# A first batch in halves of 256 tokens, early loads in another order, and a written-out list for each engine

## The chip, the cores and the metric

The kernel runs on one core of one Trainium2 chip. The metric is the device time of one execution in microseconds, the median over several. The core has a matrix engine (TensorE, PE in the profile; its weight loads are listed apart as PEld), a vector engine (DVE), a scalar engine (ACT), GpSimd (POOL) and the engine that starts most transfers (SP). Each works through its own list of instructions in order and waits on semaphores for the others. Two kinds of on-chip memory matter: SBUF, and PSUM, into which PE writes and from which DVE and ACT read.

## The reference

Attention with a feature map of exponentials, for 8 batches of 8 heads with 576 tokens of 64 features, followed by a normalised two-layer product with a residual. Cut to what matters:

```python
proj = einsum('bhsd,df->bhsf', x, w_phi)                     # 64 -> 128, for q and for k
proj = proj - max(abs(proj), axis=-1, keepdims=True)
phi  = concatenate([exp(proj), exp(-proj)], axis=-1)
kv   = einsum('bhsf,bhsd->bhfd', k_p, v);  z = sum(k_p, axis=2)
x    = einsum('bhsf,bhfd->bhsd', q_p, kv) / (einsum('bhsf,bhf->bhs', q_p, z)[..., None] + 1e-06)
x    = x.transpose(0, 2, 1, 3).reshape(8, 576, 512)
xn   = (x - mean) / sqrt(var + 1e-06) * g_ln
out  = x + maximum(xn @ w_ch1, 0.0) @ w_ch2                  # 512 -> 2048 -> 512
```

## The kernel before

**Units and groups.** The attention runs in 32 units of two heads of one batch (`NU`). Units 0 to 3 make the first 512 tokens of batch 0, units 4 to 7 those of batch 1, and so on; the last 64 tokens of each batch ("tails", "mixed", `px`) go through tiles of their own. The second part, called MoE in the code, runs over groups `g` of 512 tokens. Group 0 can start once units 0 to 3 are through. A group makes 16 first products (`first`, L1425 on: four matmuls of 512 columns into `hT_ps`, L1431, then a relu on ACT or DVE) and 4 x 16 second products (`second`, `ch_ps`, L1463). The last groups use a form with fewer multiplications (`fast`, `quick`).

**One unit.** k, q and v come in by transfers on SP. PE turns k and q (`a_trans`, L829 and L837), DVE or ACT copies them to `qkT` (L844, L846). `a_main` multiplies by `wbk`, the feature weights, with 256 columns a matmul (L984; L990 in the form for units 4 and up), DVE takes the largest absolute value over each token's 128 features (L1047, one reduction of 128 x 1024), and ACT the exponentials: for k two of 1024 into `EB` (L1067), for q two of 1024 into `EA` (L1111), the latter from a second product of q with the roles turned (`a_tails`, L999, `pt`). Small exponentials of the maxima give `ek` and `em` (L1056, L1060). `a_mixed` does the same for the 64 last tokens (`px`, L943, L944, L947, L956, L960). POOL scales v by `ek` into `vv` (L1074 to L1080), PE sums `EB` times `vv` into `n_bank` (`a_kv`, L1135, L1141), which is copied to `KV` (L1149, L1151). `a_num` multiplies `EA` by `KV` in two parts of 6 and 3 token tiles (L1199, L1205); DVE adds the two signs and takes the reciprocal of the sum (L1221, L1227, L1233), and POOL writes the quotient to `x` (L1266, L1270, "puts").

**Between the parts.** DVE takes means and variances (`x_stats` L1338, `x_center` L1350), DVE, ACT or POOL subtracts the mean (L1355, L1360, L1364), ACT makes 1/sqrt of the variance as an Ln and an Exp (`rstd`, L1370, L1371), and PE turns the result (`x_trans`, L1302) with copies on DVE or ACT (L1312, L1314). In group 0 a turn covers all four token tiles of one of four 128-wide slices, so the first product waits for all 512 tokens.

**Weights.** POOL starts the loads of w1 (L769) and w2 (L787), each in two halves, which convert to 16 bits on the way. `GATE` names the load of v that must have come before each half of w1 starts. Loads for units 8 and up wait for the half of w1 that `HOLD` names, which is half 1.

**PSUM.** Pool A has two buffers of two banks, pool B three of one bank, pool N one bank. A product waits until a buffer of its pool is free.

**The order.** Nothing is emitted as the functions run. Every function calls `add`, which records one operation: the engines that could do it, an estimate of its time, a rank, the code to emit, what it reads and writes, and which PSUM pool it takes from or gives back to. Operations are numbered in the order of these calls. At the end `Order.run` (L365 on) plays the operations through a model of the engines, picks for each free engine the waiting operation of lowest rank, and writes the instructions out in the order of that play. Ranks come from due times and from the table `OFF`, a correction for each unit and stage. While the model has no work for PE before `WARM` = 75 us, it puts in matmuls of zeros (`fill`, L2064).

## Time and profile before

| what | value |
|---|---|
| median of 3 runs | 356.31 us (356.21 to 358.39) |
| span of the profiled execution, first to last instruction | 354.4 us |
| that execution's clock of PE, as granted | 0.998 of full speed |
| transfers | 53.89 MB in 93676 packets, 152 GB/s over the span |
| bytes read and written in HBM | 36.77 MB, 9.44 MB |

The profiled execution is one run of the program. Its span reaches from the first to the last instruction, and the time of a run also holds what lies around it. A row of a timeline has the start, the duration, the engine, the line, the operation and its operands, and in brackets the idle time before it and what ended that. A row of a group has the line, engine, operation, operands, the count, the busy time, the mean duration in ns, and the idle time in front of its instructions. A row of busy time by stretch has the stretch, its length, the busy time and count of PE, PEld, DVE, ACT and POOL (those that worked), the granted clock, the share of the DMA engines and GB/s. A row of the chain has the start, the time and what it was. Instructions of one engine overlap in its pipeline, so that busy times of rows that follow each other add up to more than the time that passed.

### The profile page before, as it was taken

What the parts mean: (1) busy time and instruction counts of PE and PEld (TensorE: products, weight loads), DVE (VectorE), ACT (ScalarE), POOL (GpSimd) and SP (SyncE); (2) the same over time, 40 slices, a digit from 0 to 9 for tenths busy, and PEclk for the clock granted to TensorE, in tenths of its full rate; (3) what the DMA queues carried; (4) which work ended last, traced back from release to release, by engine and by line L of the source; (5) the groups of instructions that cost most, each with busy time, mean ns of one, the idle gap of its engine ahead of it and who ended that gap; (6) DMA issues with size and microseconds to landing.
All of it is one profiled execution on the core that took longest, in us unless ns stands there. A gap on an engine that the chain in (4) does not pass through costs nothing.

```text
span 354.4 us, 9372 instructions
## 1 busy us (share of the span) xinstructions
PE 345.6 (98%) x3606; PEld 221.1 (62%) x3632; DVE 304.8 (86%) x664; ACT 258.5 (73%) x551; POOL 189.3 (53%) x245
## 2 busy tenths in 40 slices
PE   8998999999999999999999999999999999999995
PEld 8987955556554555455545455555555578578884
DVE  5699987899987888988979989897778799999983
ACT  4997988598997996979696975787697833656410
POOL 5499755799644873747478798355546420000000
PEclk9999999999999999999999999999999999999999
DMA  7999999899996888489729242851051005400053
GB/s 210 311 215 287 210 281 246 215 235 258 294 276 175 209 185 215 115 141 280 202 68 209 72 110 47 147 153 35 2 126 63 3 7 116 123 2 3 0 120 118
DMA packets 93676, 53.89 MB, mean 152 GB/s; under 512 B 61104, under 2 KB 88048, under 8 KB 93632
## 3 DMA queue, kind: packets, MB, share of 16 engines
q1 hardware_dynamic: 89392, 47.72, 56.5%
q0 software_dynamic: 3328, 4.49, 7.1%
q10 hardware_dynamic: 912, 1.08, 0.9%
q8 instruction: 28, 0.46, 0.5%
q14 instruction: 16, 0.13, 0.1%
HBM read 36.77 MB, written 9.44 MB: 130 GB/s over the span
## 4 chain that ended last, share of the span: by engine, by line
PE 88%; DVE 8%; ACT 2%; issue 1%; DVEq 0%; ACTq 0%
PE hT_ps L1431 29%; PE ch_ps L1463 22%; PE ch L1597 9%; PE n_bank L2064 4%; PE pm L990 4%; PE n_bank L1141 4%; PE sum L1780 4%; PE num L1199 3%; PE pt L999 2%; DVE m L1047 2%; PE n_bank L1135 1%; DVE numc L1221 1%; PE n_bank L1199 1%; DVE numc L1227 1%; PE n_bank L1205 1%
## 5 line engine op out<-in xcount | busy, mean ns | idle before, releaser
L1431 PE MATMUL hT_ps<-xT,w 128*128 128x512 bf16 x496 | 118.4, 379 | 0.0
L1463 PE MATMUL ch_ps<-w,hT 128*128 128x512 bf16 x362 | 88.9, 379 | 1.3 <-issue 0.3
L1047 DVE TENSOR_REDUCE m<-pm 128x8 f32<-128x1024 f32 x64 | 76.8, 1214 | 7.1 <-PE pm L990 6.5
L1074 POOL TENSOR_TENSOR vv<-v,ek 128x1024 bf16<-128x1024 f32 x32 | 61.1, 1910 | 33.0 <-issue 18.2
L1431 PEld LDWEIGHTS <-w 128*128 128x128 bf16 x496 | 44.2, 98 | 44.0 <-issue 0.8
L1067 ACT ACTIVATE eb<-pm 128x1024 bf16<-128x1024 f32 x64 | 64.5, 1036 | 2.4 <-DVE m L1047 2.3
L1111 ACT ACTIVATE ea<-pt 128x1024 bf16<-128x1024 f32 x64 | 63.8, 1029 | 3.0 <-PE pt L999 2.7
L1266 POOL TENSOR_TENSOR x<-numc,rden 128x128 bf16<-128x128 f32 (+1 forms) x64 | 38.9, 613 | 38.6 <-DVE rden L1233 37.4
L1441 ACT ACTIVATE hT<-hT_ps 128x512 bf16<-128x512 f32 x68 | 40.6, 597 | 24.1 <-PE hT_ps L1431 23.2
L1463 PEld LDWEIGHTS <-hT 128*128 128x128 bf16 x384 | 34.0, 98 | 34.4 <-issue 0.8
L1439 DVE TENSOR_SCALAR hT<-hT_ps 128x512 bf16<-128x512 f32 x56 | 38.5, 687 | 8.6 <-PE hT_ps L1431 8.1
L1199 PEld LDWEIGHTS <-ea 128*128 128x128 bf16 x512 | 24.6, 97 | 10.5 <-issue 1.7
L1141 PE MATMUL n_bank<-vv,eb 128*128 128x65 bf16 x512 | 26.6, 194 | 0.0
L902 POOL TENSOR_TENSOR b<-qk,one 128x1024 bf16<-128x1024 f32 x11 | 20.9, 1896 | 8.9 <-DMA qkT<-b 5.5
L2064 PE MATMUL n_bank<-wz 128*128 128x120 bf16 x347 | 25.0, 224 | 0.1
L1141 PEld LDWEIGHTS <-eb 128*128 128x128 bf16 x512 | 22.3, 98 | 4.3
L1221 DVE TENSOR_TENSOR numc<-num,em 128x390 f32<-128x390 f32 (+1 forms) x40 | 20.3, 513 | 3.3 <-PE num L1199 2.5
L2064 PEld LDWEIGHTS <-wz 128*128 128x128 bf16 x347 | 21.5, 103 | 1.6 <-issue 0.5
L1480 POOL TENSOR_TENSOR o<-o,x 128x512 f32<-128x512 f32 x14 | 16.2, 1154 | 10.5 <-ACT o L1476 10.5
L1338 DVE BATCH_NORM_STATS2 st<-x 128x6 f32<-128x512 bf16 (+1 forms) x40 | 21.3, 569 | 0.4 <-POOL x L1266 0.4
L1199 PE MATMUL num<-KV,ea 128*128 128x65 bf16 x416 | 19.4, 193 | 1.6 <-ACT KV L1151 1.3
L1227 DVE TENSOR_TENSOR numc<-numc,num 128x390 f32<-128x390 f32 (+1 forms) x40 | 20.3, 516 | 0.5
(162 smaller groups left out, 608.7 us busy)
## 6 DMA issues: line engine op xcount, KB each, us to landing
out_dram<-o SPq DMA_DIRECT2D x29, 256.0 KB, 2.6
qk<-in_k_dram SPq DMA_DIRECT2D x12, 512.0 KB, 5.0
qk<-in_q_dram SPq DMA_DIRECT2D x12, 512.0 KB, 6.0
v<-in_v_dram SPq DMA_DIRECT2D x12, 512.0 KB, 4.9
w<-in_moe_w_ch_dram POOLq DMA_DIRECT2D x4, 1024.0 KB, 11.4
qk<-in_k_dram SPq DMA_DIRECT2D x8, 256.0 KB, 6.9
qk<-in_q_dram SPq DMA_DIRECT2D x7, 256.0 KB, 7.5
v<-in_v_dram SPq DMA_DIRECT2D x7, 256.0 KB, 7.4
```

The lines of the kernel that those rows point to most:

```text
L1047: nc.vector.reduce_max(out=m, in_=ps, axis=AX.X, apply_absolute_value=True)
L1067: nc.scalar.activation(eb, ps, AF.Exp, scale=(1.0, -1.0)[t])
L1074: eng.tensor_tensor(out=u["vv"][:, :, 0:MX, 0:D], in0=bcast(vb[:, hh, :].rearrange("p (c d) -> p c d", d=D), 1, 2), in1=bcast(e[:, :, 0:MX ...
L1111: nc.scalar.activation(u["EA"][:, t, 0:1024], u["pt"], AF.Exp, scale=(1.0, -1.0)[t])
L1141: nc.tensor.matmul(ps[:, t, c // 4, :], EB[:, t, c, :], vv[:, t, c, :], start=False, stop=(t == 0 and c == MX - 1), skip_group_check=True,)
L1199: nc.tensor.matmul(ps[t][:, i, :], ea(u, t, c), KV[:, t, c // 4, :], start=True, stop=True,)
L1266: eng.tensor_tensor(out=dst, in0=src, in1=by, op=ALU.mult)
L1431: nc.tensor.matmul(st["ps"], w1_sb[:, kc, jj * P : (jj + 1) * P], xT_bufs[g % XB][:, kc::KC, :], start=(kc == 0), stop=(kc == KC - 1),)
L1439: nc.vector.tensor_relu(h_sb, st["ps"])
L1441: nc.scalar.activation(h_sb, st["ps"], AF.Relu)
L1463: nc.tensor.matmul(ch[g, i], hT[g, jj][:, i * P : (i + 1) * P], w2_sb[:, jj, :], start=(jj == 0), stop=(jj == JC - 1),)
L2064: nc.tensor.matmul(warm, wz, wz[:, 0:WN], start=False, stop=False, skip_group_check=True)
```

## The change

**The order is written out.** The table `OFF` and the ranks go. In their place stands `ORDER`, which names for each engine the numbers of its operations one after the other; the model still runs, to place the filler and to merge the five lists into one program order. What `add` records for each operation is otherwise the same. The model's estimates change in many places (a table `LAG` of waits between engines, one transfer queue in place of two, other durations); they change no instruction except the number of fillers.

**Group 0 in halves.** For units 0 to 3 (`halved`), q's products go through `q_half`: two halves of 256 tokens, each with two matmuls of 256 columns in one role and two in the other in one PSUM buffer, a maximum of 128 x 512 on DVE, a small exponential and two exponentials of 512 on ACT. `num_half` takes token tiles 0, 1, 4, 5 and then 2, 3, 6, 7 with the mixed tile, in place of the parts of 6 and 3. In group 0 `x_trans_half` turns two token tiles by two slices at a time with copies of 256 columns, `rstd` is made for two tiles at a time, and `first_half` makes two first products of 256 tokens side by side in one PSUM buffer, in place of one of 512.

**Start.** Both halves of `w_phi` come by ACT's queue (one came by POOL's), q of unit 0 by SP's (it came by ACT's), the q tails of the first units are loaded as all tails are, the casts to `wbk` stand behind all the clears, and `GATE` names v of units 2 and 3 in place of 4 and 5.

The numbers of some operations of the changed kernel, counted from the calls of `add`:

| number | engine | what |
|---|---|---|
| 25 | ACT | `preload_act_table_set` |
| 85, 108, 167, 218, 273 | POOL | `vv` of units 0, 1, 2, 3, 4 |
| 154, 149 | POOL | load of w1, half 1 (slots 8 to 15) and half 0 (slots 0 to 7) |
| 168, 173 | POOL | loads of w2 |
| 130, 199, 136, 135, 205, 204, 240, 287 | POOL | puts of units 0 to 3 |
| 314, 316 | ACT, POOL | centring of token tiles 0 and 1 |
| 323, 326 | PE | `x_trans_half` of the first 256 tokens |
| 325, 327, 328, 324 | DVE, the last on ACT | their copies |
| 349, 339, 337, 343, 341 | PE | `first_half(0, 7)`, `(0, 2)`, `(0, 1)`, `(0, 4)`, `(0, 3)` |
| 374 | PE | products of q of unit 5 |
| 317, 322 | ACT | `rstd` of token tiles 0 and 1, and of 2 and 3 |
| 557, 560, 563 | PE | second products of the first token tile |
| 564 | ACT | result of the first token tile |
| 442, 465 | ACT, PE | copy of `KV` of unit 6, and the `num` that reads it |

The diff, cut to its core. The lists are cut to their first part:

```diff
-SLACK = ((0.22, 0.0, 0.0, 1.02), (0.35, 0.6, 1.6, 1.03), (0.22, -1.1, 0.0, 1.28))
+SLACK = ((0.22, 0.0, 0.0, 0.97), (0.35, 0.6, 1.6, 0.97), (0.22, -1.35, 0.0, 1.0))
...
+HALVED = 4
...
-GATE = (("v", 4), ("v", 5))
-OFF = (
...
+GATE = (("v", 2), ("v", 3))
+ORDER = {
+    "POOL": """
+        0 15 17 21 19 30 85 108 154 167 130 218 199 136 135 149 205 204 240 287 316 32 245 292
+        273 246 168 173 308 389 388 444 451 293 383 404 435 418 504 423 464 470 469 424 497 511
...
+    "SP": """
+        1 7 26 9 11 13 28 35 37 41 43 137 51 63 33 47 59 49 39 45 61 145 65 143 67 53 139 141 57
...
+    "ACT": """
+        2 72 23 98 83 99 84 93 87 94 82 119 120 97 92 79 124 106 125 105 107 118 102 123 165 166
+        164 193 194 161 192 216 215 217 188 189 187 221 212 229 230 228 278 371 234 235 233 373
+        282 413 223 314 411 271 324 272 270 267 300 350 317 377 378 338 369 331 302 303 376 275
+        305 306 307 346 362 448 364 443 447 402 356 358 403 401 409 398 352 406 429 433 434 427
+        430 432 322 564 442 25 458 459 491 457 452 575 502 494 495 496 588 526 527 524 545 599
...
+    "DVE": """
+        3 5 6 74 81 96 89 76 91 78 117 115 104 182 122 101 113 184 111 163 132 133 127 160 128
+        191 180 129 214 201 211 202 196 197 203 186 134 198 280 225 227 232 237 207 238 206 242
+        284 239 285 243 286 289 244 290 309 310 313 315 269 274 327 291 328 325 266 299 208 312
...
+    "PE": """
+        4 71 73 80 95 88 75 90 77 86 116 114 103 100 121 181 183 112 109 110 162 131 159 126 190
+        178 179 213 200 210 195 185 219 224 279 220 226 231 236 276 370 277 241 283 372 288 281
+        412 410 268 222 323 326 265 298 349 374 339 337 343 341 367 332 329 368 301 347 359 353
...
-    nc.scalar.dma_start(out=wphi_f[0:D, :], in_=w_phi)
-    nc.gpsimd.dma_start(out=wphi_f[D : 2 * D, :], in_=w_phi)
+    for i in range(2):
+        nc.scalar.dma_start(out=wphi_f[i * D : (i + 1) * D, :], in_=w_phi)
...
+    def q_half(u, h):
+        n = u["n"]
+        j = n % QB
+        st = {}
+        cs = ((0, 1, 4, 5), (2, 3, 6, 7, MX))[h]
+        nt = len(cs)
+
+        def products():
+            st["ps"] = ps = ps_A.tile([P, 2, 2, 2, P], FP32, tag="A", name="qh")
+            x = u["qkT"][:, 0:512].rearrange("p (a two t) -> p a two t", a=2, two=2)[:, :, h, :]
+            for a in range(2):
+                nc.tensor.matmul(ps[:, 0, a], x[:, a, :], wbk, start=True, stop=True)
+            for i in range(2):
+                nc.tensor.matmul(ps[:, 1, i], wbk[:, i, :], x, start=True, stop=True)
...
+    def first_half(h, j2):
+        st = {}
+
+        def products():
+            st["ps"] = ps_B.tile([P, 2, 2 * P], FP32, tag="B", name="hT_ps")
+            for k in range(2):
+                jj = 2 * j2 + k
+                for kc in range(KC):
+                    nc.tensor.matmul(
+                        st["ps"][:, k].rearrange("p (i t) -> p i t", t=P),
+                        w1_sb[:, kc, jj * P : (jj + 1) * P],
+                        xT_bufs[0][:, kc::KC, :][:, 2 * h : 2 * h + 2, :],
+                        start=(kc == 0), stop=(kc == KC - 1),
+                    )
...
-        def rstd():
-            nc.scalar.activation(rstd_x[:, g, :], mv_x[:, g, :, 1], AF.Ln, bias=eps_sb)
-            nc.scalar.activation(rstd_x[:, g, :], rstd_x[:, g, :], AF.Exp, scale=-0.5)
+        def rstd(at=slice(0, NM)):
+            nc.scalar.activation(rstd_x[:, g, at], mv_x[:, g, at, 1], AF.Ln, bias=eps_sb)
+            nc.scalar.activation(rstd_x[:, g, at], rstd_x[:, g, at], AF.Exp, scale=-0.5)
...
+        if g == 0 and i % 2:
+            add("ACT", 0.46, V, lambda: rstd(slice(i - 1, i + 1)),
+                r=[("mv", g, j) for j in (i - 1, i)], w=[("rstd", 0, i // 2)])
...
     load_main("k", 0, 1, -4.0, "SP")
-    load_main("q", 0, 1, -4.0, "ACT")
+    load_main("q", 0, 1, -4.0, "SP")
     load_tails("k", 0, -3.0, "SP")
+    load_tails("q", 0, -3.0, "POOL")
...
-            a_main(u, 0)
+            for half in range(2):
+                q_half(u, half)
```

More of the change, by code (lines that the diff above doesn't have):

```diff
@@ L393, in run @@
                 if kind == 1:
[L394 to L404 removed]
+                    offered.add(op.number)
@@ L452, in run @@
                     first, last = port[0], port[1]
-                    us = us.us + max(0.0, first - now if now < first else last - now)
-                    if now < last and any(not item[2].engine for item in waiting["POOL"]):
+                    us = us.us + max(0.0, (first if now < first else last) - now - 0.15)
+                    n = place["POOL"]
+                    if now < last and n < len(turn["POOL"]) and turn["POOL"][n] in offered:
                         us += STUCK
@@ L480, in run @@
                         offer(o)
-        assert not any(op.left or not op.engine for op in self.ops)
+        assert all(place[engine] == len(turn[engine]) for engine in turn)
         for op in done:
@@ L609 @@
         nc.vector.memset(m_, 0.0)
-    for i in range(2):
-        rows = slice(i * D, (i + 1) * D)
-        nc.vector.tensor_copy(out=wbk[rows, i, :], in_=wphi_f[rows, :])
     ea_bufs = []
```

655 lines of the change are left out of this document (286 added, 369 removed), and 99 rows, old and new, of tables (OFF, ORDER).

## The prediction

> **What bounds the kernel now.** I read the page first, then busy time by stretch, the filler's line by stretch, the chain of waits, and each engine's groups in the stretch that mattered.
>
> ```profile
> PE 345.6 (98%) x3606; PEld 221.1 (62%) x3632; DVE 304.8 (86%) x664; ACT 258.5 (73%) x551; POOL 189.3 (53%) x245
> ```
>
> PE looks full everywhere, but part of it is filler (L2064 multiplies zeros to pass the time). The first fence splits the span of 354.4 us where the first MoE product starts; the second is the filler alone in the same stretches.
>
> ```profile
> 0.00:44.60 44.60, 41.24 (x727) 38.14 (x732) 37.53 (x96) 36.57 (x83) 31.55 (x50) 1.00 1.09 246
> 44.60:354.40 309.80, 304.34 (x2880) 182.96 (x2900) 267.24 (x569) 221.97 (x470) 157.79 (x196) 1.00 0.59 138
> ```
>
> ```profile
> 0.00:44.60 44.60, 24.53 (x345) 21.30 (x345) 1.00 1.09 246
> 44.60:354.40 309.80, 0.43 (x2) 0.20 (x2) 1.00 0.59 138
> ```
>
> The columns after the stretch are PE, PEld, DVE, ACT, POOL. Before 44.6 us PE has 24.5 us of filler and 3.4 idle; after it, 0.4 and 5.5, most of that behind the last matmul. So two different bounds: up to 44.6 us PE waits for the first batch to come through DVE (37.5 of 44.6 busy) and ACT (36.6); from 44.6 on PE's own work sets the end. The chain shows the border (start, time, what):
>
> ```profile
> 43.71 0.11 PE px L943
> 43.82 0.06 PE px L944
> 43.87 0.55 PE pm L990 x16
> 44.43 0.16 PE n_bank L2064
> 44.59 0.86 PE hT_ps L1431 x4
> 45.45 0.06 PE n_bank L1135
> 45.51 0.26 PE n_bank L1141 x8
> ```
>
> Hence the sum: the new span is the start S of the first MoE product plus the PE work that is left then, plus whatever new waits appear behind S.
>
> **The change: work left at S.** The new PE list puts 54 operations ahead of its first half product (number 349, `first_half(0, 7)`). I compare them with what PE had done by 44.59 us:
>
> ```profile
> L1199 PE MATMUL num<-KV,ea 128*128 128x65 bf16 x80 | 4.3, 194 | 1.6 <-ACT KV L1151 1.3 <-ACT ea L1111 0.3
> L1141 PE MATMUL n_bank<-vv,eb 128*128 128x65 bf16 x80 | 4.0, 194 | 0.0
> L990 PE MATMUL pm<-wbk,qkT 64*128 64x128 bf16 x48 | 2.0, 217 | 0.0
> L1205 PE MATMUL num<-KV,ea 128*128 128x65 bf16 x20 | 1.8, 193 | 0.0
> L1302 PE MATMUL xT_ps<-ident,xc 128*128 128x128 bf16 x16 | 1.2, 219 | 0.0
> ```
>
> Means overlap in the pipeline, so prices come from the chain's spacing: 8 of L1141 take 0.26 (0.033 each), a 128-wide one 0.06 (L944), a 256-wide 0.11 (L943), a 512-wide 0.215 (4 of L1431 in 0.86), and L990 0.034 (16 in 0.55). By 44.59 PE had five units' num and kv; the new list has four, so 20 + 16 of 0.033 and two wider ones are still to do (1.3 us). It has one group of 16 L990 in place of three (1.1 us) and 8 transposes of x in place of 16 (0.45 us). That is 2.8 us more behind S. The halves turn 64 matmuls of 512 columns (13.8 us) into 128 of 256 (14.1 us): 0.2 more. Left behind S: 309.8 + 2.8 + 0.2 = 312.8, with the old idle and the old tail in it. Both loads of `w_phi` on ACT, the clears ahead of the casts and the preset costs in the planner change no work behind S.
>
> **When S comes: DVE.** DVE's groups up to 44.59 us:
>
> ```profile
> L1047 DVE TENSOR_REDUCE m<-pm 128x8 f32<-128x1024 f32 x13 | 15.7, 1214 | 0.5 <-PE pm L984 0.5
> L1227 DVE TENSOR_TENSOR numc<-numc,num 128x195 f32<-128x195 f32 (+1 forms) x10 | 4.4, 453 | 0.1
> L1221 DVE TENSOR_TENSOR numc<-num,em 128x195 f32<-128x195 f32 (+1 forms) x10 | 4.3, 449 | 0.1
> ...
> L947 DVE TENSOR_REDUCE m<-px 128x2 f32<-128x256 f32 x7 | 2.9, 421 | 1.0 <-PE px L944 1.0
> L1338 DVE BATCH_NORM_STATS2 st<-x 128x6 f32<-128x256 bf16 x8 | 2.9, 408 | 0.0
> L1233 DVE RECIPROCAL rden<-numc 128x3 f32<-128x3 f32 (+1 forms) x10 | 1.5, 174 | 0.0
> L1312 DVE TENSOR_SCALAR xT<-xT_ps,ngln 128x512 bf16<-128x512 bf16 x3 | 1.3, 478 | 0.1
> ```
>
> Ahead of the last copy that number 349 needs, the new DVE list has 6 whole maxima and 8 half ones (half of 1.214 and a little, 0.65) in place of 13: 3.3 us less. Eight pairs of numc and 8 rden in place of ten: 2.15 less. Four px maxima for seven: 1.25. Four stats for eight, since tokens 256 to 511 come later: 1.65. Three half copies of xT (0.3) for three whole: 0.5. Together 8.85; neighbours overlap by some 0.09 and 12 instructions fewer lose that, so 7.8, and 8.3 with small copies. That alone moves 44.6 to 36.3. DVE's gaps early on can shrink as well:
>
> ```profile
> 5.00:10.00 5.00, 4.95 (x82) 4.66 (x81) 3.82 (x9) 2.96 (x5) 0.70 (x1) 1.00 1.06 263
> 10.00:15.00 5.00, 4.95 (x79) 4.55 (x78) 3.19 (x6) 4.88 (x16) 2.61 (x3) 1.00 1.11 305
> ```
>
> 3.0 us idle there; SP now issues k and q of units 0 to 3 ahead of every v but unit 0's. No row prices that: between nothing and 3.0, I take a third. First half product: **35.3 us**. ACT's halved exponentials add some 0.3 us a unit and sit beside DVE.
>
> **When S comes: the weights.** Number 349 reads the half of w1 that POOL now loads first; the second operation behind it (339) reads the other half.
>
> ```profile
> 22.05 0.63 POOL L1080 TENSOR_TENSOR vv<-vx,ek 128x260 bf16<-128x260 f32 x1
> ...
> 24.29 1.18 POOL L1266 TENSOR_TENSOR x<-numc,rden 128x384 bf16<-128x384 f32 x2 [0.86 <-DVE rden L1233]
> ...
> 25.68 1.91 POOL L1074 TENSOR_TENSOR vv<-v,ek 128x1024 bf16<-128x1024 f32 x1
> ...
> 27.68 0.62 POOL L1080 TENSOR_TENSOR vv<-vx,ek 128x260 bf16<-128x260 f32 x1
> 28.24 0.79 POOL L769 DMA_DIRECT2D w<-in_moe_w_ch_dram  x1
> ```
>
> ```profile
> DMA to landing us min/median/max: 9.9/10.0/10.1
> ```
>
> POOL's list keeps the places: one half behind the second vv, one behind the fourth and the puts after it. A vv takes 2.6 us (25.68 to 28.3); the puts now ahead of the second half take 1.4 (two large ones took 1.18, and a small one). If the fourth vv follows the third at once (22.65), that half is issued at 26.6; with today's gaps at 28.24 + 1.4 = 29.6. With 10.0 us to land: 36.6 to 39.6. I take 36.6, since the exponentials that vv waits for also come earlier. In the meantime PE does 349 and 374 (0.86 + 0.44), so this too puts S at **35.3**. The two limits meet. w2 is issued behind five more puts, a centring and the vv of unit 4, at about 35 us by these rows and later if that vv waits for ACT; it is due behind 16 half products of 0.88 and some 4.5 us of attention work (an estimate by the same prices), at 53. A landing of 10.0 hides in that; I cost it at nothing, and one us for each us that it lands later.
>
> **A wait that the change adds.** Operation 25, the preload of ACT's tables, ran ahead of all activations. The ACT list now has it behind 97 others, both early rstd among them (numbers 317 and 322, each a Ln and then an Exp).
>
> ```profile
> 2.47 1.28 ACT L1966 ACT_TABLE_LOAD   x1 [2.47 <-issue]
> 4.54 0.58 ACT L846 COPY qkT<-qkT_ps 128x512 bf16<-128x512 bf16 x1 [0.78 <-PE qkT_ps L829]
> ```
>
> ```profile
> 44.60:60.00 15.40, 15.40 (x146) 8.52 (x146) 11.69 (x20) 12.79 (x29) 8.76 (x12) 1.00 1.22 280
> ```
>
> Something must then load tables for the first activation, and if that set has only Exp, each rstd switches twice: 4 x 1.28 = 5.1 us on ACT between the first product and the first second product. Queued behind 322 are the result of the first tile, which frees a PSUM buffer, and the KV copy of unit 6, which PE's num of unit 6 waits for. ACT had 15.40 - 12.79 = 2.6 us idle in that stretch, so 2.5 reach PE. Ends: 0 (one load serves all) and 4 x 2.07 = 8.3 (from the load's start at 2.47 to ACT's next work at 4.54) less 2.6, so 5.7. I take 2.5, by the load's own row. The Trainium skill ("ScalarE: Activation LUTs", Table sets: the hidden batching unit) lists a set with exp alone beside one with exp and ln, and says that a load is placed before an activation whose function is not loaded; by that the four switches happen, while the trace of before, with one load ahead of everything, can't show it. The same page (What ACT_TABLE_LOAD costs) gives 1.28 us for the load, as the row has it, and 2.66 with a drain; by 2.66 the sum below would be 358.0 instead of 352.5.
>
> **Sum.** 35.3 + 312.8 + 2.5 = 350.6 us of span. The profiled execution has 354.4 against the median of 356.31, so 1.9 lie around it: **352.5 us**, 1.1% below. One per cent (3.6 us) is about what a measurement of this kernel tells from no change.
>
> **The rivals.**
> 1. The tables cost PE nothing, because one set serves or ACT loads while PE waits for w1: 35.3 + 312.8 + 1.9 = 350.0; with DVE's whole early gap closed (2 us more, weights keeping up) 348.0. For it: ACT's 2.6 us of idle time; against it: the two rstd stand ahead of the preload.
> 2. Each switch holds ACT longer than its row, up to the 2.07 above: 350.0 + 5.7 = 355.7, within 1%. PE then waits longer at num of unit 6. The Trainium skill's page "ScalarE: Activation LUTs" (What ACT_TABLE_LOAD costs) has such a time as a drain.
> 3. Slower: the second half of w1 is late. Both halves of w2 went through the same queue behind another weight:
>
> ```profile
> DMA to landing us min/median/max: 12.8/15.6/18.3
> ```
>
> With 18.3 the half lands at 44.9, S is 43.6 and the time 43.6 + 312.8 + 2.5 + 1.9 = 360.8. It turns slower than before where the landing takes over 13.8 us. For it: loads of units 8 and up wait for the first half and now start beside the second; against it: both w1 halves took 10.0 beside other loads.
> 4. The change does nothing for S: PE, DVE and ACT wait for each other in new places of the fixed lists, and S stays above 40. Then 357 and more. Against it: DVE's list is 8.3 us shorter.
>
> **How the numbers follow.** Forecast (351 to 354.5) 0.45; rival 1 (348 to 351) 0.27; rival 2 (354.5 to 357.5) 0.14; rival 3 (over 357.5) 0.09; rival 4 (357 to 360) 0.05. The range 348 to 357.5 leaves out rival 3 and most of rival 4, and a little below. Faster by over 1% means under 352.75: rival 1 and about 0.55 of the forecast, 0.52. Slower by over 1% means above 359.9: half of rival 3 and a little of 4, 0.06. Within 1%: 0.42.
>
> **What would show it.** Right: the first hT_ps at 34 to 37 us and filler down by 8 to 10 us, almost none behind it. DVE up to there at about 27 us of work beside the clears. Four table loads between 35 and 62 us, and PE idle at num of unit 6 beside them. Wrong: PE waiting behind its first half product for the second half of w1 beyond 38 us (rival 3); a single early table load (rival 1); fillers and gaps of DVE behind S, or a first product above 40 us (rival 4).

## The result, and the profile after

| | before | after |
|---|---|---|
| median | 357.26 us (356.21 to 358.39, 4 runs) | 361.09 us (359.67 to 362.8, 4 runs) |
| ratio | | 1.0121, 95% interval 1.0075 to 1.0168 |
| span of the profiled execution | 354.4 us | 360.1 us |
| its clock of PE | 0.998 | 0.995 |

The change made the kernel 1.2% slower, where 1.1% faster was forecast. The first line of the page of after looks much like the one of before:

```profile
PE 345.5 (96%) x3579; PEld 223.1 (62%) x3579; DVE 298.8 (83%) x667; ACT 258.9 (72%) x567; POOL 193.0 (54%) x251
```

PE is busy for the same 345 us, in a span that is 5.7 longer. Busy time by stretch, cut at the start S of the first MoE product (columns as before: PE, PEld, DVE, ACT, POOL), and under it the filler's line alone:

```profile
0.00:39.63 39.63, 33.43 (x531) 30.64 (x532) 30.00 (x81) 28.62 (x71) 22.32 (x37) 1.00 0.97 224
39.63:360.10 320.47, 312.11 (x3052) 192.47 (x3048) 268.79 (x587) 230.30 (x497) 170.67 (x215) 0.99 0.61 140
```

```profile
0.00:39.63 39.63, 17.59 (x222) 15.12 (x222) 1.00 0.97 224
```

Filler fell by 6.9 us (24.5 to 17.6), where 8 to 10 were forecast, and DVE's work up to S is the 27.5 us beside 2.5 of clears that were forecast as about 27. But S came at 39.6 us, 5.0 earlier than before and not at 35.3. (Of the kernel before, the chain has S at 44.59 and the timeline, from which S is read in all other runs, at 44.42, so that a split at S is good to 0.2 us.) Behind it lie 320.5 us in place of the 315.3 that were forecast (312.8, and 2.5 for the tables). So there are two misses, of 4.3 and of 5.2 us. The second is easy to see in PE's timeline of after:

```profile
39.63 1.04 PE L1358 MATMUL hT_ps<-xT,w 128*128 128x256 bf16 x8
...
41.72 3.67 PE L1358 MATMUL hT_ps<-xT,w 128*128 128x256 bf16 x32 [0.51 <-DMA w<-in_moe_w_ch_dram]
...
47.50 0.61 PE L1327 MATMUL xT_ps<-ident,xc 128*128 128x128 bf16 x8 [1.80 <-ACT hT L1372]
...
69.78 0.27 PE L1197 MATMUL num<-KV,ea 128*128 128x65 bf16 x2 [2.00 <-ACT KV L1149]
...
70.50 2.75 PE L1533 MATMUL ch_ps<-w,hT 128*128 128x512 bf16 x6
...
73.45 1.46 PE L1533 MATMUL ch_ps<-w,hT 128*128 128x512 bf16 x6
```

The brackets hold the idle time and who ended it: twice ACT, once a weight load. The last two rows are a second sign: six matmuls of 512 columns take 2.75 at first, and another six of the same size 1.46 three us later. ACT's timeline shows what it did ahead of the first of these waits:

```profile
41.35 0.66 ACT L1372 ACTIVATE hT<-hT_ps 128x512 bf16<-128x512 f32 x1
42.03 1.28 ACT L1437 ACT_TABLE_LOAD   x1
43.33 0.30 ACT L1437 ACTIVATE rstd<-mv,eps 128x2 f32<-128x2 f32 x1
43.64 1.28 ACT L1438 ACT_TABLE_LOAD   x1
44.94 0.20 ACT L1438 ACTIVATE rstd<-rstd 128x2 f32<-128x2 f32 x1
```

Two table loads around one small rstd, and the same again at 65.79 and 67.39, with the late preload at 69.75. The clock that PE was granted (third number from the end), in stretches of 5 us and, in the second fence, of 2.5:

```profile
65.00:70.00 5.00, 3.00 (x42) 1.56 (x39) 2.55 (x5) 4.92 (x10) 4.10 (x5) 0.97 1.08 260
70.00:75.00 5.00, 5.00 (x39) 2.36 (x38) 2.22 (x6) 4.72 (x10) 1.50 (x2) 0.69 0.17 38
```

```profile
70.00:72.50 2.50, 2.50 (x14) 1.17 (x12) 0.98 (x3) 2.49 (x3) 1.50 (x2) 0.50 0.35 76
72.50:75.00 2.50, 2.50 (x26) 1.19 (x26) 1.24 (x3) 2.23 (x8) 0.00 (x0) 0.88 0.00 0
```

Behind the wait of 2.00 us the clock is half of the full one for some three us, 0.69 in the mean of five; that is 1.6 us lost (5.00 times 0.31, an estimate). Of the four runs, those with a mean clock of 1.0 have spans of 357.9 and 358.5, the others 360.1 and 361.0.

The first miss, the late start, shows in DVE's waits up to 40 us (what waited, for whom: us in total, times, longest):

```profile
DVE wbk L490 <- DMA wphi_f<-in_w_phi_dram: 2.9, 2, 2.0
DVE m L871 <- ACT ea L885: 2.4, 3, 1.1
DVE qkT L716 <- PE qkT_ps L701: 1.8, 2, 1.1
```

The second line is new: DVE's half maximum waits for ACT's half exponential. DVE's busy time (third of the busy columns) in the first 15 us, before and after:

```profile
0.00:15.00 15.00, 13.90 (x196) 13.22 (x199) 8.54 (x27) 9.58 (x21) 7.17 (x15) 1.00 0.91 245
```

```profile
0.00:15.00 15.00, 11.29 (x120) 10.21 (x121) 6.51 (x24) 5.54 (x8) 4.05 (x11) 1.00 0.96 247
```

DVE has 2.0 us more idle time there, where the prediction had expected a little less than before.

### The profile page after: what moved, and what is told of

Its sections match the earlier page's. It is cut to its first block, busy times and chain, and to the rows that moved or that the text cites. A ratio compares the mean times of both kernels' runs of the same rounds, so it can differ in the third digit from the quotient of the medians.

```text
span 360.1 us, 9262 instructions
## 1 busy us (share of the span) xinstructions
PE 345.5 (96%) x3579; PEld 223.1 (62%) x3579; DVE 298.8 (83%) x667; ACT 258.9 (72%) x567; POOL 193.0 (54%) x251
## 4 chain that ended last, share of the span: by engine, by line
PE 85%; ACT 8%; DVE 4%; DMA 1%; issue 1%; SPq 0%
PE hT_ps L1501 26%; PE ch_ps L1533 22%; PE ch L1669 10%; PE pm L988 4%; PE n_bank L1139 4%; PE sum L1852 3%; PE num L1197 3%; PE hT_ps L1358 2%; PE pt L997 2%; DMA qk<-in_q_dram 1%; ACT eb L1065 1%; ACT ea L885 1%; PE n_bank L2141 1%; PE n_bank L1133 1%; DVE m L871 1%; PE n_bank L1197 1%
## 5 line engine op out<-in xcount | busy, mean ns | idle before, releaser
L1501 PE MATMUL hT_ps<-xT,w 128*128 128x512 bf16 x432 | 102.8, 379 | 0.0
L1045 DVE TENSOR_REDUCE m<-pm 128x8 f32<-128x1024 f32 x60 | 72.1, 1213 | 9.3 <-PE pm L988 8.8
L1501 PEld LDWEIGHTS <-w 128*128 128x128 bf16 x432 | 38.8, 98 | 40.2 <-issue 1.6
L1109 ACT ACTIVATE ea<-pt 128x1024 bf16<-128x1024 f32 x56 | 55.8, 1040 | 4.4 <-PE pt L997 4.4
L1511 ACT ACTIVATE hT<-hT_ps 128x512 bf16<-128x512 f32 x59 | 34.3, 611 | 12.7 <-PE hT_ps L1501 12.6
L1509 DVE TENSOR_SCALAR hT<-hT_ps 128x512 bf16<-128x512 f32 x49 | 32.9, 681 | 4.7 <-PE hT_ps L1501 4.6
L1219 DVE TENSOR_TENSOR numc<-num,em 128x390 f32<-128x390 f32 (+1 forms) x32 | 17.0, 532 | 10.7 <-PE num L1197 7.0
L829 ACT ACTIVATE eb<-n_bank 128x128 bf16<-128x128 f32 x48 | 13.7, 286 | 8.7 <-DVE m L820 8.7
L1078 POOL TENSOR_TENSOR vv<-vx,ek 128x260 bf16<-128x260 f32 x32 | 20.0, 624 | 0.0
L988 PEld LDWEIGHTS <-qkT 64*128 64x128 bf16 x448 | 13.7, 94 | 9.7 <-issue 7.5
L988 PE MATMUL pm<-wbk,qkT 64*128 64x128 bf16 x448 | 19.7, 217 | 0.0
```

Source lines behind the costliest of these rows:

```text
L988: nc.tensor.matmul(ps[:, half * 4 + c, :], u["qkT"][rows, cols], wbk[rows, half, :], start=True, stop=True,)
L1045: nc.vector.reduce_max(out=m, in_=ps, axis=AX.X, apply_absolute_value=True)
L1109: nc.scalar.activation(u["EA"][:, t, 0:1024], u["pt"], AF.Exp, scale=(1.0, -1.0)[t])
L1501: nc.tensor.matmul(st["ps"], w1_sb[:, kc, jj * P : (jj + 1) * P], xT_bufs[g % XB][:, kc::KC, :], start=(kc == 0), stop=(kc == KC - 1),)
L1511: nc.scalar.activation(h_sb, st["ps"], AF.Relu)
```

## The experiments

All changes are against the kernel after, except in E4. "S" is the start of the first MoE product in the run's profile. It is one execution's: after, E12 and E1, whose work up to there differs by the preload alone, have 39.63, 39.61 and 39.20. Ratios are to the kernel before on the same chip, whose medians were 357.26 us beside the kernel after and 356.65 to 356.76 beside the experiments. In the table a name such as E5 in front of an edit means that run with one more edit.

| run | S, us | median, us | ratio, 95% interval |
|---|---|---|---|
| after | 39.6 | 361.09 | 1.0121 (1.0075 to 1.0168) |
| E1 tables first | 39.2 | 355.83 | 0.9967 (0.9954 to 0.9979) |
| E2 early loads back, tables late | 39.1 | 361.68 | 1.0131 (1.0102 to 1.0159) |
| E3 the edits of E1 and E2 | 38.8 | 361.36 | 1.0134 (1.0113 to 1.0156) |
| E4 before, tables late | 47.5 | 359.97 | 1.0087 (1.0056 to 1.0118) |
| E5 E1, half maximum first | 40.7 | 356.63 | 1.0000 (0.9987 to 1.0014) |
| E6 E3, another place in ACT's list | 39.9 | 355.66 | 0.9975 (0.9950 to 1.0000) |
| E7 E5, w1's second half early | 40.5 | 356.81 | 0.9999 (0.9986 to 1.0012) |
| E8 E7, early loads back | 39.6 | 356.19 | 0.9982 (0.9966 to 0.9999) |
| E9 E1, stand-in maximum | 38.1 | 355.23 | 0.9954 (0.9940 to 0.9969) |
| E10 E1, no fillers | 39.0 | 355.89 | 0.9979 (0.9962 to 0.9997) |
| E11 the edits of E9 and E10 | 36.7 | 354.21 | 0.9938 (0.9917 to 0.9960) |
| E12 after, PE kept busy | 39.6 | 361.16 | 1.0120 (1.0096 to 1.0145) |
| E13 E1, own tile, no fillers | 39.0 | 355.33 | 0.9955 (0.9940 to 0.9971) |
| E14 E1, own tile, fewer fillers | 37.2 | 354.82 | 0.9942 (0.9927 to 0.9957) |
| E15 E1, fewer fillers | 38.7 | 354.77 | 0.9942 (0.9928 to 0.9957) |
| E16 E14, early loads back | 37.2 | 354.06 | 0.9927 (0.9912 to 0.9941) |

### The tables: E1, E4, E12

**E1.** The preload goes back to the front of ACT's list.

```diff
     "ACT": """
-        2 72 23 98 83
+        2 25 72 23 98 83
...
-        430 432 322 564 442 25 458 459
+        430 432 322 564 442 458 459
```

> The changed kernel with one edit: the preload of ACT's tables stands second in ACT's list again instead of 98th. Theory A (table switches): the four loads at the two rstd and the late preload are gone, so are PE's waits of 1.80 and 2.00 us at 45.7 and 67.8 us, and the slow matmuls behind 70 us (some 1.7 us); the first MoE product stays at 39.6 us, and the time falls from 361.1 by 4 to 5.5 us, to 355.6 to 357. Rival B (the fixed lists themselves, or the halves, cost the time): the loads go, but PE waits at other places, and the time falls by less than 1.5 us. Rival C (the clock fell for its own reasons): the two waits go and the slow stretch stays, so the time falls by about 3.8 us and PE's clock is under 0.8 in some 5 us near 70.

355.83 us: theory A. ACT's timeline has the first rstd without loads (0.6 us in all, where it took 3.1):

```profile
41.40 0.36 ACT L1436 ACTIVATE rstd<-mv,eps 128x2 f32<-128x2 f32 x1
41.79 0.20 ACT L1437 ACTIVATE rstd<-rstd 128x2 f32<-128x2 f32 x1
```

Both of PE's waits for ACT and the slow stretch are gone; S hardly moved. One number in one list was worth 1.5% (1.0121 to 0.9967). What is left of the change is 0.3% faster than before, where 1.1% was forecast with the tables in the sum, so the start is still to be explained.

**E4.** The kernel before, with the set that lacks Ln loaded early and the joint one at the second group's rstd.

```diff
-        lambda: nc.scalar.preload_act_table_set("natural_log_exp_and_others"),
+        lambda: nc.scalar.preload_act_table_set("exp_and_others"),
...
         def rstd():
+            if g == 1:
+                nc.scalar.preload_act_table_set("natural_log_exp_and_others")
```

> The kernel before, with ACT's early preload loading the set that has Exp without Ln, and the joint set loaded only ahead of the second group's rstd. So the rstd of the first group, near 42 us, switches tables twice and the second one once: three loads of 1.28 us more, nothing else moved. Theory A (a switch there reaches PE): ACT's results behind 42 us come 2.6 us later, the first MoE product moves from 44.6 to 45.5 to 47, and the time rises by 1 to 3.5 us. Rival (ACT's slack hides switches, and the changed kernel is slow for other reasons): within 0.7 us of the kernel before.

359.97 us, 3.2 above the kernel before: the switch costs there too. S moved to 47.5, a little beyond the 47 that was expected. ACT's and PE's timelines and the clock by stretch:

```profile
42.82 1.28 ACT L1372 ACT_TABLE_LOAD   x1
44.11 0.30 ACT L1372 ACTIVATE rstd<-mv,eps 128x4 f32<-128x4 f32 x1
44.42 1.28 ACT L1373 ACT_TABLE_LOAD   x1
```

```profile
46.89 0.61 PE L990 MATMUL pm<-wbk,qkT 64*128 64x128 bf16 x8 [2.25 <-ACT eb L1067]
```

```profile
45.00:47.50 2.50, 0.61 (x9) 0.41 (x9) 0.91 (x1) 2.49 (x6) 1.06 (x3) 0.87 1.23 196
47.50:50.00 2.50, 2.50 (x15) 1.31 (x16) 1.22 (x1) 1.13 (x6) 0.00 (x0) 0.50 1.19 258
```

PE waited 2.25 us and then had half of its clock. The four runs split again: 360.9 and 361.0 us with a mean clock of 0.995 and 0.993, 358.8 and 359.1 with 0.998 and 0.999. So in these two kernels a wait of two us has two prices, itself and some 2 us of slow clock, and the second isn't charged every time.

**E12.** The changed kernel, with eight products of zeros ahead of PE's second wait.

```diff
             for jj in range(j0, j0 + n):
...
+            if (g, i, j0) == (0, 1, 0):
+                for _ in range(8):
+                    nc.tensor.matmul(ch[g, i], wz, w2_sb[:, 0, :], start=False, stop=False)
```

> The changed kernel as it is, tables late, with eight more products of zeros (512 columns, 1.7 us together) added into the second token tile's sum just ahead of PE's wait of 2.00 us at 67.8. They change no result. If PE's clock fell to 0.69 behind that wait because PE stood idle, it now stays at 0.97 or above in 70 to 75 us, num of unit 6 starts at the same 69.8, and the time is 0.5 to 1.7 us less than the changed kernel's, 359.4 to 360.5, with less spread between runs. If the clock has other reasons, the slow stretch stays and so does the time, within 0.4.

PE's timeline and the clock show what was expected for the place itself, num of unit 6 at the same time and the full clock behind it:

```profile
67.62 1.89 PE L1539 MATMUL ch_ps<-w,wz 128*128 128x512 bf16 x8
69.80 0.22 PE L1197 MATMUL num<-KV,ea 128*128 128x65 bf16 x2 [0.29 <-ACT KV L1149]
```

```profile
70.00:75.00 5.00, 4.95 (x69) 3.03 (x67) 3.78 (x10) 4.99 (x10) 2.70 (x5) 1.00 0.04 9
```

But the time is the changed kernel's, 361.16, and two of its four runs still have a mean clock of 0.993 and 0.994. The other wait, at 45.1 us, was not filled. In the profiled execution it is 2.39 us long, and the clock stays full behind it:

```profile
47.50 0.61 PE L1327 MATMUL xT_ps<-ident,xc 128*128 128x128 bf16 x8 [2.39 <-ACT hT L1372]
```

```profile
47.50:50.00 2.50, 2.50 (x38) 2.10 (x38) 1.86 (x4) 1.55 (x4) 0.00 (x0) 1.00 1.19 237
```

This execution has a span of 358.5, in line with the executions of the changed kernel at a full clock (357.9 and 358.5). Of the other three no trace was kept; two of them have the same span, 359.4, with mean clocks of 1.0 and 0.994. The expectation for the time failed, and what took the place of the gain stays open.

### What did not hold the start: E2, E3, E6, E7, E8

**E2, E3 and E6.** q of unit 0 back on ACT's queue and the second half of `w_phi` back on POOL's; E3 and E6 with the tables first as well.

```diff
-    for i in range(2):
-        nc.scalar.dma_start(out=wphi_f[i * D : (i + 1) * D, :], in_=w_phi)
+    nc.scalar.dma_start(out=wphi_f[0:D, :], in_=w_phi)
+    nc.gpsimd.dma_start(out=wphi_f[D : 2 * D, :], in_=w_phi)
...
-    load_main("q", 0, 1, -4.0, "SP")
+    load_main("q", 0, 1, -4.0, "ACT")
...
-ACT: 2 72 23 ...    SP: 1 7 26 9 11 13 ...
+E2: ACT: 2 9 72 23 ...    E3: 2 25 9 72 23 ...    E6: 2 9 25 72 23 ...    SP: 1 7 26 11 13 ...
```

> The changed kernel with the early loads back where they were: q of unit 0 on ACT's queue instead of third on SP's, and the second half of w_phi on POOL's queue instead of ACT's. The table loads stay late. Theory A (late start): the second half of wbk is cast near 5.2 instead of 6.49 us, the first k product comes near 5.6 instead of 7.50 and its maximum near 6.6 instead of 8.60; the first MoE product moves from 39.6 to 37.2 to 38, and the time falls by 1.6 to 2.4 us, to 358.7 to 359.5. Rival B (waits for each other further on in the lists set the start): the first maximum moves but the first MoE product stays above 39.2, and the time changes by less than 0.5. Rival D (the second half of w1 is the limit): the first MoE product moves, and PE waits as much longer for that half, which lands near 41.2 in the changed kernel.

> The changed kernel with both edits: tables loaded at the front, and q of unit 0 and the second half of w_phi back on their old queues. Theory A, both causes independent: the sum of the two savings, 353.5 to 355, which is 0.6 to 1.1 per cent below the kernel before. Rival B: not below the kernel before. If the earlier start only runs into the second half of w1, the time is that of the run with the tables alone, 355.6 to 357.

> The changed kernel with tables, q of unit 0 and the second half of w_phi back, as in the run that had both, but with q's issue written ahead of the table load in ACT's list. By the planner's clock that lets q land earlier, so it writes 14 fillers behind the first MoE product in place of 116. If those fillers were what made that run slow, the time falls from 361.36 to 355 to 356.2; the first maximum of DVE comes by 7.8 instead of 8.7, the first MoE product at 38.2 to 39 and PE waits (or fills) up to 41.3 for w1. If the early loads themselves were at fault, the time stays above 359.

E2's first maximum of DVE came at 7.67 in place of 8.60 us (6.6 was expected), S moved by 0.5, to 39.1, and the time not at all: rival B, whose bound for S was 39.2. Part of that 0.9 may be chance: E12, with the same work up to there as the kernel after, had its first maximum at 7.90 and S at 39.61. E3 was a surprise, 5.5 us slower than E1. PE's timeline of E3:

```profile
38.78 1.04 PE L1356 MATMUL hT_ps<-xT,w 128*128 128x256 bf16 x8
39.75 0.40 PE L986 MATMUL pm<-wbk,qkT 64*128 64x128 bf16 x8
39.98 0.38 PE L995 MATMUL pt<-qkT,wbk 64*128 64x512 bf16 x2
40.30 6.26 PE L2139 MATMUL n_bank<-wz 128*128 128x120 bf16 x116
46.40 0.82 PE L1356 MATMUL hT_ps<-xT,w 128*128 128x256 bf16 x6
```

These 116 products of zeros are not a wait. By its own clock the planner saw a pause there and wrote them into PE's list, and PE must work through them although w1's second half had landed by 41.5 us (issued at 30.79, at most 10.7 us to landing). In E6 the same operations with q's issue one place earlier give 14 such products, and 355.66 us, no better than E1. Its time is as expected, but S came at 39.9, where 38.2 to 39 were expected. So the early loads, an obvious suspect by the trace, are not what the start waits for.

**E5, E7 and E8.** Each keeps E1's tables. In E5 the half maximum takes its turn ahead of ACT's exponential: the order in which the five lists are merged decides who waits for whom at a PSUM tile. E7 adds w1's second half earlier in POOL's list, E8 the early loads of E6 too.

```diff
-        add("DVE", 0.6, rk("q.max", n), maxima,
+        first = add("DVE", 0.6, rk("q.max", n), maxima,
...
-        add("ACT", 0.494, rk("tails.exp", n), lambda: exps(0),
+        later = add("ACT", 0.494, rk("tails.exp", n), lambda: exps(0),
...
+        later.behind = first
...
-POOL: ... 154 167 130 218 199 136 135 149 205 ...
+E7, E8: ... 154 167 149 130 218 199 136 135 205 ...
```

> The changed kernel with the tables loaded at the front (355.83 us, first MoE product at 39.20) and one more edit: DVE's half maximum of q takes its turn at the shared PSUM tile ahead of ACT's first half exponential, in place of behind it. Each engine's list of instructions and the 223 fillers stay as they are, only the waits between DVE and ACT change. Theory F (DVE's idle time early on is the taking of turns at that tile): DVE's waits for ACT at the half maximum, 2.4 us in three places, go; the first MoE product moves to 37 to 38.3. The second half of w1 lands near 41.5 as before, so PE's wait there grows from 0.74 to 1.5 to 2.5 us and the time falls by 0 to 1 us only, to 354.8 to 355.8. Rival G (ACT then waits as long for the maximum and hands it on): the first MoE product within 0.4 of 39.2 and the time within 0.5.

> As the run with the half maximum first and the tables at the front, and w1's second half issued by POOL right behind the vv of unit 2, ahead of unit 3's vv and of four puts. Theory D (the second half of w1 is the limit as soon as the rest is early): it is issued near 26 instead of 31.5 and lands by 37, PE's wait for it goes, and the first MoE product stays where that run has it; 0.7 to 2.5 us less than that run, 353 to 354.6. Rival (POOL's later vv and puts, or two weight loads side by side, hold DVE and PE up as long): within 0.5 us of that run.

> All four edits: tables at the front, q of unit 0 and the second half of w_phi back on their queues, the half maximum first, w1's second half early. If the causes add up: the first MoE product at 36 to 37.5, no wait for w1, and 352 to 353.8 us, about 1 per cent below the kernel before. If DVE's work from 15 us on already decides, the first MoE product is within 0.4 of the run without the early loads and so is the time.

E5: DVE's wait for ACT went, and the start got 1.5 us later; rival G and worse. ACT's waits up to 40 us show where it went, 8.9 us for DVE, where E1 had 1.6 for DVE and 5.4 for PE:

```profile
ACT ea L919 <- DVE m L905: 8.9, 5, 5.7
```

ACT then gives the tile back later, and PE's next products wait for the tile (1.3 us for ACT's `ea`, where E1 has 0.3). Changing whose turn it is does not help while both need the same tile. E7: PE's wait for w1 (0.78 in E5) goes, and the median does not fall (356.81). So w1's second half is not the limit, at least not alone. E8 brings the first maximum to 7.36 and S to 39.6, and its median is 0.6 us below E7's, with intervals that overlap; the 36 to 37.5 that were expected for S if the causes add up were missed.

### What held it: E9, E10, E11, E13 to E16

**E9.** The half maximum reads a constant of the same size, so that the tile is ACT's alone; q's maximum is then another number in units 0 to 3. **E10.** No fillers by the planner. **E11.** Both.

```diff
-                in_=st["ps"][:, 0].rearrange("p a i f -> p (a i) f"),
+                in_=bcast(wphi_f[:, :], 1, 4),
...
-WARM = 75.0
+WARM = 0.0
```

> The changed kernel with the tables loaded at the front (355.83 us, first MoE product at 39.20). DVE's half maxima of q read w_phi, a constant in SBUF with as many elements, in place of the PSUM tile that ACT's half exponentials read too, so the stabiliser of q is another one in the first four units; lists and fillers stay as they are. Theory F (DVE and ACT take turns at the tile of the half products): the waits of DVE for ACT and of ACT for DVE there (2.4 and 1.6 us) go, and the first MoE product moves by 1 to 2.4 us, to 36.8 to 38.2; PE then waits longer for w1's second half, so the time falls by less, 354 to 355.5. Rival H (PE's fixed list with its written fillers, and the two large PSUM tiles, hold the first units back): DVE's waits turn into waits for PE, and the first MoE product stays within 0.5 of 39.2.

> The changed kernel with the tables at the front and without the planner's fillers: PE's list has 11 of the products of zeros in place of 223, all in the first two us. Rival H (fillers that the planner wrote by its own clock stand ahead of work that is ready): DVE's waits for PE at qkT_ps and qxT_ps (1.8 us) shrink, and the first MoE product comes 1 to 2.5 us earlier, at 36.7 to 38.2. Theory F: within 0.5 of 39.2. If PE's clock needs the fillers, it is under 0.9 in stretches ahead of the first product and the products take longer, so the first MoE product comes later, above 40.

> The two runs above in one: tables at the front, half maxima of q from w_phi, no fillers by the planner. If F and H each hold a part of the early idle time, the first MoE product comes at 35 to 37, near the 35.3 that was predicted, and w1's second half (41.3) sets the rest. If it stays above 38.7, neither is what holds the first units, and what is left are the two large PSUM tiles and the order of the lists.

E9: S moves by 1.1 us, to 38.06, in the range of theory F. DVE's waits for ACT at the maximum are gone, and a part of the gain was handed on, since DVE's wait for PE at `qkT`, 1.4 us in E1, grew:

```profile
DVE qkT L715 <- PE qkT_ps L700: 2.7, 2, 1.4
```

E10: S by 0.2 only, within theory F's 0.5, but the clock falls in a stretch where PE pauses, and with it the products slow down; busy time by stretch:

```profile
20.00:25.00 5.00, 4.18 (x57) 3.31 (x54) 4.06 (x10) 4.28 (x15) 4.33 (x7) 0.66 1.13 299
```

E11, in a profiled execution with the full clock, has the first product here:

```profile
36.68 1.03 PE L1357 MATMUL hT_ps<-xT,w 128*128 128x256 bf16 x8
```

That is 2.5 us earlier than E1. Together they do more than the sum of the two, 1.1 and 0.2. One reading is that with the tile free, fillers stand ahead of ready work, and with the fillers gone, the tile does. But that is argued, not shown: E10's execution had the slow clock (its first MoE product took 1.91 us, E11's 1.03). And E11 reads other values, and a start without fillers hangs on the clock.

**E13 to E16.** The half maximum gets a bank of its own from pool B and reads the true products; the planner counts that bank and gives it back behind the maximum. E14 to E16 have fewer fillers, by making the model count one as two: E14 has 156 products of zeros and E15 119, where E1 has 223. E13 has only the 11 of the start. E15 keeps the shared tile. E16 adds the early loads.

```diff
             st["ps"] = ps = ps_A.tile([P, 2, 2, 2, P], FP32, tag="A", name="qh")
+            st["qm"] = qm = ps_B.tile([P, 2, 2, P], FP32, tag="B", name="qm")
...
-                nc.tensor.matmul(ps[:, 0, a], x[:, a, :], wbk, start=True, stop=True)
+                nc.tensor.matmul(qm[:, a], x[:, a, :], wbk, start=True, stop=True)
...
-                in_=st["ps"][:, 0].rearrange("p a i f -> p (a i) f"),
+                in_=st["qm"].rearrange("p a i f -> p (a i) f"),
...
-    sched.filler = ("PE", WARM, mm(1, WN), fill)
+    sched.filler = ("PE", WARM, 2 * mm(1, WN), fill)
```

> The changed kernel with the tables at the front; the half maximum of q comes from a one-bank PSUM tile of its own, the half exponentials from the other, so both read at will and the result is the reference's; no fillers by the planner. If the shared tile and the fillers hold the start (F and H): the first MoE product at 36.3 to 37.8, as with the stand-in (36.68), and 353.7 to 355. If the bank that is taken from the other small tiles costs as much as it frees, it stays above 38.3.

> As the run with the tile of its own, with about half as many fillers as there are pauses for by the planner's clock (151 in place of some 300), so that PE is never idle long but reaches ready work sooner. F and H together: the first MoE product at 36.5 to 38, PE's clock at 1.0 throughout, 353.6 to 355.0. If only the absence of fillers frees it: above 38.3.

> The changed kernel with the tables at the front and half of the fillers (119 in place of 223); the tile stays shared. H alone: the first MoE product at 38.2 to 39.2 and 355 to 355.9, which is 0 to 0.8 us below the run with the tables alone. F alone: no change, 39.2 and 355.8.

> As the run with a tile of its own and half of the fillers, with q of unit 0 and the second half of w_phi back on their old queues. If the early loads count once nothing else holds the first units: the first maximum 1 us earlier than there, the first MoE product 0.4 to 1 us earlier, the time 0.3 to 0.8 us less. If not, the two are the same within 0.4 us.

E13 missed: S at 39.0, with PE's clock at 0.80 and 0.86 in the ten us from 20 on. E14 hit: S 37.2, clock 1.0 up to S. Its timelines of DVE and of ACT show the two reading the products of one half at the same time, 9.4 to 10.1:

```profile
9.37 0.68 DVE L875 TENSOR_REDUCE m<-qm 128x4 f32<-128x512 f32 x1
```

```profile
9.48 0.60 ACT L889 ACTIVATE ea<-qh 128x512 bf16<-128x512 f32 x1 [4.59 <-PE qh L872]
```

And busy time by stretch shows DVE back at the 8.5 us of work in the first 15 that the kernel before had, and what is left behind S:

```profile
0.00:15.00 15.00, 10.85 (x110) 9.27 (x111) 8.65 (x28) 7.39 (x17) 4.68 (x12) 1.00 0.94 249
```

```profile
0.00:37.16 37.16, 30.12 (x459) 26.05 (x460) 29.90 (x81) 28.39 (x71) 22.37 (x37) 1.00 1.01 237
37.16:353.00 315.84, 309.40 (x3035) 192.01 (x3053) 268.52 (x587) 223.90 (x492) 171.00 (x215) 1.00 0.62 143
```

Of the 2.0 us that S gains on E1, 1.2 arrive in the profiled span (354.2 to 353.0): PE now waits 0.7 for w2 within the first second product, the transfer that had been hidden. E15 moves S by 0.5 and its median is as low as E14's (354.77, below the 355 to 355.9 that were expected), so in the time the tile and the fillers can't be told apart: E14 and E15 agree within their intervals, and only S and DVE's idle time ahead of it separate them (7.3 us in E14, 9.1 in E15). Against E1 the intervals of both just touch; of E13 to E16 only E16's lies clear of it. E16 gives 354.06 us, 0.7% below the kernel before and 2% below the changed one. Its S is E14's (37.24 and 37.16, where 0.4 to 1 us earlier was expected), so what the early loads bring there (0.8 us, with overlapping intervals) is not shown to be theirs. In its profile PE does not wait for w2, which is 0.7 of the 0.9 us between the two spans.

## Why the prediction was wrong, point by point

Two steps failed. The wait that the tables add was put at 2.5 us and cost 5.3, without which the change is 0.3% faster than before (E1). The start S was put at 35.3 and came at 39.6, since DVE's idle time ahead of it, which the step let shrink, grew.

**"Span is the start S plus the work left behind it": right.** In the twelve runs with early tables other than E3, S lay between 36.7 and 40.7 us and the span less S between 314.2 and 315.8.

**"A wait that the change adds": right mechanism, too small a size.** The four loads came at the two rstd, and the late preload made a fifth; PE's second wait was at num of unit 6, as forecast. The step subtracted ACT's 2.6 us of idle time, summed over 15 us, from the loads. But idle time elsewhere in a stretch cannot be used by an instruction that stands in a queue behind a load. PE waited 1.80, at a place that the text did not name, and 2.00, so 3.8 in place of 2.5 us. The clock behind these waits was not in the sum at all: about 2 us between the halves of the four runs, 1.6 by the stretch from 70 to 75. E1 gives the whole price, 5.3 us. Rival 2 had the direction, with a longer load as its reason; the load was not longer. Its 2.07 was a misreading: the load ends at 3.75 (2.47 + 1.28), and the 0.78 up to 4.54 is, by the bracket of the row, a wait for PE. The Trainium skill ("ScalarE: Activation LUTs", What ACT_TABLE_LOAD costs) adds a drain of 1.38 us to a load of 1.28. The trace has the 1.28 and no drain: the load starts 0.02 us behind the end of ACT's row ahead of it (41.35 + 0.66, and 42.03), and Ln 0.02 us behind the load's end (42.03 + 1.28, and 43.33). The Trainium skill ("ScalarE: Activation LUTs", Table sets: the hidden batching unit) counts one load for an Ln and the Exp behind it, since one set has both. By that count there would be fewer than the four switches that the prediction drew from this section. The trace has a load ahead of the Ln and another ahead of the Exp each time (42.03 and 43.64, 65.79 and 67.39, and 42.82 and 44.42 in E4), and in E1, with the joint set loaded ahead of all, none there. So the four came as forecast, but the section does not account for them.

**"When S comes: DVE": the work right, the idle time wrong.** The step had 29.2 us of DVE work ahead of S (37.5 less 8.3); it was 30.0. But it also took "a third" of 3.0 us of early gaps as closed, and its bounds there, "between nothing and 3.0", allow only for a gain; that DVE's gaps could grow was not considered. DVE's idle time ahead of S rose from 7.1 (44.6 less 37.5) to 9.6 us. The half products put what DVE and ACT read into one PSUM buffer, where the maximum of q and its exponentials had had one each; the diff showed that, and the text named it, but the sentence "ACT's halved exponentials add some 0.3 us a unit and sit beside DVE" took it for granted that both can read at once. With a tile of its own for the maximum and fewer fillers (E14), the idle time is 7.3 us again and S 37.2. Of the 4.3 us that S was late, 2.0 went with E14's two edits (39.2 in E1 to 37.2), and 0.4 lie between the kernel after and E1, which the early preload or chance may have made. Of the rest 0.7 is more work than counted and 1.2 the gaps that never closed. How the 2.0 divide between tile and fillers is not settled: alone, E9 moved S by 1.1 and E15 by 0.5.

**"When S comes: the weights": the rows right, no limit.** The halves of w1 were issued at 22.8 and 31.6, where the step had taken 26.6, out of 26.6 to 29.6, for the second; PE waited 0.5 us for it. E7, with the load issued 5.4 us earlier than in E5 (27.3 and 32.8) and no wait, was no faster, so rival 3 falls. w2 was issued at 43.1, not at about 35, and cost the changed kernel no wait, as the step had it.

**"Work left at S": too small by 1.5.** In E1 315.0 less its wait of 0.74 for w1 is 314.3, which is 4.5 above the 309.8 of before (4.3 with S from the timeline in both); forecast was 3.0. Left out were operations that PE had done by 44.6 and now does later, two of these `pt`: 56 matmuls of 512 columns stand behind S in place of 52 (4 of 0.215 make 0.9), and three px in place of one (2 of 0.17, 0.3). The groups of PE behind S, in E1 and before:

```profile
L996 PE MATMUL pt<-qkT,wbk 64*128 64x512 bf16 x56 | 10.8, 381 | 0.0
```

```profile
L999 PE MATMUL pt<-qkT,wbk 64*128 64x512 bf16 x52 | 10.0, 381 | 0.0
```

**The rivals.** Rival 4 said that engines would wait for each other in new places of the fixed lists, with S above 40; that was half of the truth (S 39.6, one such place at the shared tile) and got a chance of 0.05, because "DVE's list is 8.3 us shorter" was held against it, which says nothing of waits. The sum over the misses of the profiled execution: 4.3 for S, 1.3 for ACT's waits, 0.5 for w1, 1.5 for work. The 1.9 that are left of 9.5 are close to the 1.6 of the slow clock.

## What to carry to other kernels

When a change puts two readers' data into one PSUM buffer, or moves an instruction behind others on its engine, write down for each pair who must wait for whom; a shorter list of work moves a start only if these waits do not grow. Idle time of an engine, summed over a stretch, pays for nothing that stands behind a blocking instruction. And products that fill an engine's pauses are written by a model's clock: they hold back ready work when the model is late (116 of them, 6.3 us, in E3), and cost the clock when they are missing (E10, E13), so a thinner dose is worth a run.

## What the hardware showed that was not expected

**The clock falls behind short waits, and not always.** PE's clock was 0.50 over 2.5 us behind a wait of 2.00 us in the changed kernel and behind one of 2.25 in E4, while E2's profile has a wait of 2.0 at the same num and a mean clock of 0.998, and E12's has the longest, 2.39, with a clock of 1.00 behind it. The Trainium skill ("TensorE: Matmul & The Clock Gate", What's actually happening) has PE at half its clock after an idle window of about 3.4 us that runs freely. The half clock agrees with the runs, and so does the element of chance, though no run here shows the window; here pauses of two us were enough.

**Two engines can read two banks of PSUM side by side.** The shared buffer has two banks, and the maximum and the exponentials read different ones; DVE waited for ACT by a semaphore that the program's order put there for the whole buffer; with the order turned (E5), ACT waited for DVE. The Trainium skill ("PSUM — Partial Sum Buffer", PSUM bank collisions raise a hardware error) asks for such a wait within one bank. E14, where the halves lie in two tiles, agrees: both engines read at once at 9.4 us, at the usual 0.68 and 0.60 us.
